# Cosine attention and a gated matmul pair: quad 3's transposes between M1's blocks, quad 4's ahead of quad 7's loads, the last tile in 512 and 256 columns

## Chip, cores, metric

One NeuronCore of one Trainium2 chip. The metric is device microseconds of one execution, the median of several runs. The profile is of one execution; its times count from the first instruction.

## The reference

```python
batch, n_heads, seq, head_dim = (8, 12, 448, 64)
n_tokens, d_model, d_ff = (3584, 768, 2048)

q_n = q / (np.linalg.norm(q, axis=-1, keepdims=True) + 1e-06)
k_n = k / (np.linalg.norm(k, axis=-1, keepdims=True) + 1e-06)
scores = np.matmul(q_n, k_n.transpose(0, 1, 3, 2)) / tau
scores = scores - np.max(scores, axis=-1, keepdims=True)
attn = np.exp(scores)
attn = attn / (np.sum(attn, axis=-1, keepdims=True) + 1e-09)
attn_out = np.matmul(attn, v)
x = attn_out.transpose(0, 2, 1, 3).reshape(B * S, H * D)   # 3584 x 768
h = x @ w_in                                               # 3584 x 2048
g = h * np.cos(h)
out = g @ w_out                                            # 3584 x 768
```

Inputs and output are float32.

## The kernel before

The twelve heads of a batch are taken four at a time; such a group is a *quad*, three to a batch, 24 in all. For a quad, q and k are loaded (`load_qk`, on SP's queue), squared and summed (`square`), turned into inverse norms (`inverse`: Ln and Exp on ScalarE, a reduce and a reciprocal on VectorE), scaled to bf16 (`scale`, into the single buffers `Qn` and `Kn`), and transposed into `qT` and `kT`. The first quads (0 to 3) are transposed on TensorE (`transpose`: seven 128x128 transposes into one PSUM bank, then one copy to SBUF on VectorE or ScalarE); from quad 4 on SP issues two transposing DMAs (`turn`). `scores` then makes one of seven groups of a quad's scores in a pair of PSUM banks, ScalarE takes the exponential into `E`, `attend` multiplies with v. The sums of E for quads 3 to 5 are spread over all partitions by a matmul (`spread`, L622) and inverted by Ln and Exp on ScalarE; later quads sum in rounds of two (`round_`, L661) and spread by DMA. The result is `xT`, the transposed input of the second half, one per batch.

The second half of a batch is M1 and M2. **M1** (`m1_part`, L707): eight pairs of 128 columns of `w_in`; each pair has two blocks of six matmuls of 448 columns, one block to a bank. `m1` then computes h cos h of the pair: ScalarE rounds h/2pi to an integer (L720), VectorE reduces the argument (L722), ScalarE takes the sine (L724), VectorE multiplies (L726) into `gT`. **M2** (`m2`, L735): a tile of 128 tokens has two halves of 384 output columns, each 16 matmuls, then one copy on VectorE (L744) and the store on SP (the last tile: on SP and ScalarE's queue, half by half).

The attention of later quads is spread over the M2 of a batch: `VISITS[c]` lists, for batch c, how many score or attend slots come next and how many M2 matmuls after them. `begin(qd)`, called at the first scores of a quad, normalises quad qd+2, turns it, loads quad qd+4 and squares quad qd+3.

TensorE's order is the order of the program (`key`, moved by `MOVE`; `FILL` puts small products on the identity into it, L846 and L850, at given operation numbers). Up to `P.strict = False` the order of the other engines is written out too. After that a planner chooses, at each free moment of an engine, among the instructions that are ready by its own durations: the one whose result TensorE needs first, with `lead` as an advantage in us. All waits are on semaphores by the tiles read and written; a PSUM bank is one such tile, so a writer waits for all readers of the whole bank. Two instructions marked `lock` are not planned at the same time.

W2 (`w_out`) is loaded in four chunks on GpSimd's queue (chunk i holds the blocks f = 4i to 4i+3 that M2 needs); `half[3]` holds the loads of the last two. PSUM has 8 banks: M1 of batch 0 uses, pair by pair, the banks `at_bank = 2, 0, 6, 4, 2, 6, 0, 4` and the one after each. The buffers for q and k in float32 are three each (quad modulo 3), `qT` and `kT` three each.

Of the kernel before, what the change touches and what calls it, by code (L numbers as in the profile page):

```python
# [21 lines left out]
class Planner:  # L22
# [81 lines left out]
    FILL = {24: [13, 1, 'f'], 42: [3, 1, 'f'], 56: [9, 1, 'q'], 137: [1, 6, 'q'], 139: [10, 6, 'q'], 141: [4, 2,  # L104
            'q'], 155: [6, 6, 'q'], 157: [5, 6, 'q'], 246: [2, 2, 'f'], 312: [1, 0, 'f']}
# [180 lines left out]
def bass_cosine_attention__then__act_gcu_kernel(  # L286
# [216 lines left out]
    def scale(qd, w, eng="pool", part=ALL[0]):  # L503
# [4 lines left out]
        return op(eng, (1.05 if eng == "dve" else 1.65) * (j1 - j0) / NJ,  # L508
                  lambda e: e.tensor_tensor(n[0].ap()[:, j0:j1].rearrange("p j r d -> p r j d"), f[s].ap()[:, :, j0:j1],  # L509
                                            rb, ALU.mult),  # L510
                  r=cut(nm + "f", s, part) + cut("rr%d" % w, u, part), w=cut(nm + "n", 0, part), lock=True)
# [19 lines left out]
    def transpose(qd, which, bk, part=ALL[0], eng="dve"):  # L531
        u = qd % 3
        j0, j1 = part
        n, t, nm = ((Qn, qT, "Q"), (Kn, kT, "K"))[which]

        def mm(e):
            for j in range(j0, j1):
                ins = e.transpose(PS.ap()[:, 512 * bk + 64 * j:512 * bk + 64 * j + 64].bitcast(BF16),
                                  n[0].ap()[:, j], ident.ap())
            return ins  # L540

        op("pe", 0.057 * (j1 - j0), mm, r=cut(nm + "n", 0, part) + ["ident"], w=whole(bk))
        src = PS.ap()[:, 512 * bk + 64 * j0:512 * bk + 64 * j1].bitcast(BF16)
        dst = t[u].ap()[:, j0:j1].rearrange("p j a x -> p (j a x)")
        if eng == "act":
            op("act", 0.13 + 0.067 * (j1 - j0), lambda e: e.activation(dst, src, ACT.Copy), r=whole(bk), w=cut(nm + "T", u, part))  # L546
            return
        op("dve", 0.07 + 0.067 * (j1 - j0), lambda e: e.tensor_copy(dst, src), r=whole(bk),
           w=cut(nm + "T", u, part))

    def turn(qd, after=()):

        u = qd % 3
        for n, t, nm in ((Qn, qT, "Q"), (Kn, kT, "K")):
            op("sp", 1.3, lambda e, n=n, t=t: e.dma_start_transpose(  # L555
                t[u].ap().rearrange("p j a x -> p j (a x)"), n[0].ap().rearrange("p j r d -> p (j r d)")),
               r=cut(nm + "n", 0, ALL[0]), w=cut(nm + "T", u, ALL[0]), dma=(nm + "T", u), moves=1.1, packet=18,
               after=after)

# [154 lines left out]
    def m1(c, pr, bk):  # L714
        s = pairs[0] % 3
        pairs[0] += 1
        col = S * (c % 2)
        bs = pair(bk)

        op("act", 0.815, lambda e: e.activation(ar[s].ap().bitcast(I32), two(bk), ACT.Identity, bias=0.25, scale=INV2PI),  # L720
           r=bs, w=[("ar", s)])
        op("dve", 1.005, lambda e: e.scalar_tensor_tensor(ar[s].ap(), ar[s].ap().bitcast(I32), -2.0 * math.pi, two(bk),  # L722
                                                          ALU.mult, ALU.add), r=bs + [("ar", s)], w=[("ar", s)])
        act("sin", 0.86, lambda e: e.activation(ar[s].ap(), ar[s].ap(), ACT.Sin, bias=GUARD * math.pi / 2.0, scale=GUARD),  # L724
            r=[("ar", s)], w=[("ar", s)])
        op("dve", 1.01, lambda e: e.tensor_tensor(gT.ap()[:, 2 * pr:2 * pr + 2, col:col + S], two(bk), ar[s].ap(), ALU.mult),  # L726
           r=bs + [("ar", s)], w=[("g", c % 2, 2 * pr), ("g", c % 2, 2 * pr + 1)])

    def m2(t, h, f0, f1, bk):
        col = 128 * t % GC  # L730
        bs = sorted({(128 * t) // S % 2, (128 * t + 127) // S % 2})

        def mm(e):
            for f in range(f0, f1):
                ins = e.matmul(bank(bk, HW), gT.ap()[:, f, col:col + 128], W2.ap()[:, f, HW * h:HW * h + HW],  # L735
                               start=(f == 0), stop=(f == NNB - 1))
# [4 lines left out]
        if f1 == NNB:
            so = t % 3
            end = t == B * S // 128 - 1
            op("dve", 0.475, lambda e: e.tensor_copy(osb[so].ap()[:, HW * h:HW * h + HW], bank(bk, HW)),  # L744
               r=whole(bk), w=[("o", so, h)])
            if end:
                store(t, HW * h, HW * h + HW, [("o", so, h)], ("sp", "act"))
# [35 lines left out]
    put_off = []  # L783

    def begin(qd):
# [5 lines left out]
        if qd < NQ - 4:  # L791
            steps.append(lambda after=(): load_qk(qd + 4, after))
# [329 lines left out]
```

## Time and profile before

| | |
|---|---|
| Median of 3 runs | 421.54 us (421.14 to 423.64) |
| Profiled execution | 422.46 us, span 420.6 us |
| TensorE busy | 410.1 us, 97% of the span |
| ScalarE, VectorE, GpSimd busy | 308.0, 271.6, 203.2 us |
| Matmuls M1 (L707) | 768, 146.8 us busy |
| Matmuls M2 (L735) | 896, 156.3 us busy |
| Read from HBM, written | 45.61 MB, 11.01 MB |

A row of a timeline gives the start in us, the length, the engine, the line of the kernel, the operation, what it writes and reads, its shape, how many are merged, and in brackets the idle time of the engine ahead of it with what ended that. PE is TensorE, PEld its weight loads, DVE is VectorE, ACT ScalarE, POOL GpSimd, SP SyncE; a q behind the name is that engine's queue. A row of groups gives busy time in us, the mean of one in ns, and the idle time ahead. The ends of matmuls are modelled, so that neighbours overlap a little.

M1 of batch 0 runs on TensorE from 35.02 us on, the visits of batch 0 from 59.34, M1 of batch 1 from 89.10.

### The profile page before, as it was taken

To read this page: it belongs to the slowest core of one execution; us is meant where nothing else is said; L and a number is where in the kernel's file an instruction comes from. 1 tells how busy PE (TensorE), PEld (TensorE's weight loads), DVE (VectorE), ACT (ScalarE), POOL (GpSimd) and SP (SyncE) were. 2 spreads that over 40 slices of the span, in tenths; PEclk is the share of its full clock that TensorE was granted. 3 is DMA by queue.
4 is the path that set the end of the run, shared out by engine and by line. 5 is a ranking of instruction groups with operands and counts; after the bars stand their busy time and mean duration, and the time that the engine had idled before them with its cause. 6 is when DMAs were issued, how large, how long until landed. Compare 5 with 4: busy or idle time off the path is not lost.

```text
span 420.6 us, 8751 instructions
## 1 busy us (share of the span) xinstructions
PE 410.1 (97%) x3700; PEld 219.2 (52%) x3700; DVE 271.6 (65%) x339; ACT 308.0 (73%) x412; POOL 203.2 (48%) x138
## 2 busy tenths in 40 slices
PE   7999999999999999999999999999999999999996
PEld 6564454445554455445555555454554555555563
DVE  5857796889863659845985469824883137836931
ACT  5998888988888977788788657789787747505700
POOL 2867337893286982689538763359303213000000
PEclk9999999999999999999999999999999999999999
DMA  8999999896099998499909991389605633031033
GB/s 261 230 241 210 232 216 250 210 206 153 2 204 167 246 258 221 73 191 205 258 25 206 183 269 40 61 145 228 144 0 83 134 71 86 2 75 39 1 75 76
DMA packets 71400, 62.84 MB, mean 149 GB/s; under 512 B 40512, under 2 KB 66368, under 8 KB 71360
## 3 DMA queue, kind: packets, MB, share of 16 engines
q1 hardware_dynamic: 60688, 50.09, 51.3%
q0 software_dynamic: 10240, 11.80, 17.4%
q8 instruction: 29, 0.48, 0.5%
q10 hardware_dynamic: 432, 0.39, 0.3%
q14 instruction: 11, 0.09, 0.1%
HBM read 45.61 MB, written 11.01 MB: 135 GB/s over the span
## 4 chain that ended last, share of the span: by engine, by line
PE 80%; DMA 11%; POOL 2%; DVE 2%; ACT 2%; SPq 1%; issue 1%
PE PS L735 33%; PE PS L707 30%; DMA W<-in_moe_w_out_dram 8%; PE PS L573 7%; PE PS L600 6%; PE PS L661 3%; DMA Qf<-in_q_dram 3%; SPq L555 1%; POOL E L461 1%; ACT E L581 1%; POOL W L436 1%; DVE n L465 1%; DVE AVs L609 1%; POOL sqq L461 0%; DVE osb L744 0%
## 5 line engine op out<-in xcount | busy, mean ns | idle before, releaser
L735 PE MATMUL PS<-W,gT 128*128 128x384 bf16 x896 | 156.3, 327 | 0.0
L581 ACT ACTIVATE E<-PS 128x896 bf16<-128x896 f32 x161 | 136.7, 917 | 20.0 <-PE PS L573 19.3
L707 PE MATMUL PS<-xT,W 128*128 128x448 bf16 x768 | 146.8, 353 | 0.3 <-ACT qT L546 0.3
L735 PEld LDWEIGHTS PS<-W,gT 128*128 128x128 bf16 x896 | 83.4, 98 | 69.4 <-issue 16.4
L707 PEld LDWEIGHTS PS<-xT,W 128*128 128x128 bf16 x768 | 74.7, 98 | 70.4 <-issue 0.6
L720 ACT ACTIVATE ar<-PS 128x896 int32<-128x896 f32 x64 | 58.2, 911 | 40.7 <-PE PS L707 40.5
L722 DVE SCALAR_TENSOR_TENSOR ar<-ar,PS 128x896 f32<-128x896 int32 x64 | 69.2, 1084 | 22.2 <-ACT ar L720 22.0
L726 DVE TENSOR_TENSOR gT<-PS,ar 128x896 bf16<-128x896 f32 x64 | 69.5, 1088 | 7.8 <-ACT ar L724 7.4
L744 DVE COPY osb<-PS 128x384 f32<-128x384 f32 x56 | 31.1, 555 | 65.1 <-PE PS L735 64.4
L724 ACT ACTIVATE ar<-ar 128x896 f32<-128x896 f32 x64 | 60.5, 947 | 15.4 <-DVE ar L722 15.2
L461 POOL TENSOR_TENSOR sqq<-Qf 128x896 bf16<-128x896 f32 x21 | 35.7, 1698 | 43.6 <-DVE n L465 30.2
L685 POOL TENSOR_TENSOR xT<-AVs,R 128x896 bf16<-128x896 f32 x17 | 35.5, 2088 | 41.4 <-DMA R<-Zs 41.3
L509 POOL TENSOR_TENSOR Qn<-Qf,rr 128x896 bf16<-128x896 f32 x21 | 37.9, 1806 | 32.5 <-DVE rr L501 21.4
L573 PE MATMUL PS<-qT,kT 64*64 64x448 bf16 x672 | 49.1, 358 | 2.6 <-ACT E L581 1.2
L461 POOL TENSOR_TENSOR sqk<-Kf 128x896 bf16<-128x896 f32 x21 | 37.3, 1778 | 8.0 <-DMA Kf<-in_k_dram 4.9
L600 PE MATMUL PS<-E,Vb 64*64 64x448 bf16 x672 | 37.7, 351 | 0.0
L609 DVE COPY AVs<-PS 128x896 f32<-128x896 f32 x21 | 22.9, 1090 | 19.5 <-PE PS L600 19.4
L465 DVE TENSOR_REDUCE n<-sqq 128x14 f32<-128x896 bf16 (+2 forms) x23 | 23.8, 1036 | 12.8 <-POOL sqq L461 12.0
L509 POOL TENSOR_TENSOR Kn<-Kf,rr 128x896 bf16<-128x896 f32 x18 | 30.4, 1687 | 0.6 <-DMA kT<-Kn 0.6
L573 PEld LDWEIGHTS PS<-qT,kT 64*64 64x64 bf16 x672 | 16.6, 105 | 26.4 <-issue 10.0
L421 POOL DMA_DIRECT2D Vb<-in_v_dram x24 | 17.9, 750 | 17.2 <-PE PS L573 11.8
L600 PEld LDWEIGHTS PS<-E,Vb 64*64 64x64 bf16 x672 | 19.2, 107 | 13.1 <-ACT E L581 1.8
(57 smaller groups left out, 212.8 us busy)
## 6 DMA issues: line engine op xcount, KB each, us to landing
out_dram<-osb SPq DMA_DIRECT2D x54, 192.0 KB, 3.3
Qf<-in_q_dram SPq DMA_DIRECT2D x23, 448.0 KB, 5.2
Kf<-in_k_dram SPq DMA_DIRECT2D x23, 448.0 KB, 5.4
R<-Zs SPq DMA_DIRECT2D x72, 112.0 KB, 3.5
Vb<-in_v_dram POOLq DMA_DIRECT2D x24, 224.0 KB, 7.0
W<-in_moe_w_in_dram POOLq DMA_DIRECT2D x4, 768.0 KB, 18.2
W<-in_moe_w_out_dram POOLq DMA_DIRECT2D x4, 768.0 KB, 26.8
qT<-Qn SPq DMA_TRANSPOSE x20, 4.3
```

The costliest lines, as they stand in the source:

```text
L461: op(eng, (1.68 if eng == "pool" else 1.05) * n, lambda e: e.tensor_tensor(dst, src, src, ALU.mult), r=cut(nm + "f", s, part), w=own, afte ...
L509: lambda e: e.tensor_tensor(n[0].ap()[:, j0:j1].rearrange("p j r d -> p r j d"), f[s].ap()[:, :, j0:j1], rb, ALU.mult),
L573: ins = e.matmul(bank(bs + r, S, 64 * a, 64 * a + 64), kT[u].ap()[64 * r:64 * r + 64, j, a, :], qT[u].ap()[64 * r:64 * r + 64, :, a, :], s ...
L581: act("exp", 0.81, lambda e: e.activation(E[es].ap(), two(bs), ACT.Exp, bias=0.0, scale=INV_TAU), r=pair(bs), w=[("E", es)], chain="E")
L600: ins = e.matmul(bank(bk + a, S, 64 * r, 64 * r + 64), Vb[vs].ap()[64 * a:64 * a + 64, r, j, :], E[es].ap()[64 * a:64 * a + 64, r, :], sta ...
L685: op(*(("dve", 1.05) if qd == 8 else ("pool", 2.04)), lambda e, u=u, sl=sl, b=b, c0=c0: e.tensor_tensor(xT[b % 2].ap()[:, c0:c0 + 2, :], A ...
L707: ins = e.matmul(bank(bk + i2), W1.ap()[:, i, 128 * nb:128 * nb + 128], xT[c % 2].ap()[:, i, :], start=(i == 0), stop=(i == NKC - 1))
L720: op("act", 0.815, lambda e: e.activation(ar[s].ap().bitcast(I32), two(bk), ACT.Identity, bias=0.25, scale=INV2PI), r=bs, w=[("ar", s)])
L722: op("dve", 1.005, lambda e: e.scalar_tensor_tensor(ar[s].ap(), ar[s].ap().bitcast(I32), -2.0 * math.pi, two(bk), ALU.mult, ALU.add), r=bs ...
L724: act("sin", 0.86, lambda e: e.activation(ar[s].ap(), ar[s].ap(), ACT.Sin, bias=GUARD * math.pi / 2.0, scale=GUARD), r=[("ar", s)], w=[("a ...
L726: op("dve", 1.01, lambda e: e.tensor_tensor(gT.ap()[:, 2 * pr:2 * pr + 2, col:col + S], two(bk), ar[s].ap(), ALU.mult), r=bs + [("ar", s)] ...
L735: ins = e.matmul(bank(bk, HW), gT.ap()[:, f, col:col + 128], W2.ap()[:, f, HW * h:HW * h + HW], start=(f == 0), stop=(f == NNB - 1))
```

## The change

Quad 3's transposes stood together ahead of pair 3's blocks, in pair 3's own banks, both copied by ScalarE. Now Q's stand between pair 2's blocks, in bank 4, copied by VectorE, and K's between pair 3's blocks, in bank 3, copied by ScalarE. Q of quad 3 is scaled on VectorE ahead of K on GpSimd, and the inverse norms of quad 4 come before both in the program, with a lead of 30; in M1 of batch 0 the last two steps of each pair have a lead of 1. Quad 4's transposing DMAs wait for the first of W2's last two chunks, no longer for both, and quad 7's loads wait until quad 4's K transpose has landed. The last tile's output is made as 512 and 256 columns. Further edits: `VISITS`, two `FILL` entries, the `MOVE` numbers that the reordering shifts.

```diff
-            119: 3.5, 197: 41.0, ...
+            119: 3.5, 197: 36.0, ...
-     ... 212: 17.5, 90: 3.5, 218: 4.0, 210: 5.5, ... 211: -2.0,
+     ... 210: 19.5, 90: 3.5, 218: 4.0, 208: 7.5, ... 209: -2.0,
-            'q'], 155: [6, 6, 'q'], 157: [5, 6, 'q'], 246: [2, 2, 'f'], 312: [1, 0, 'f']}
+            'q'], 155: [6, 6, 'q'], 157: [5, 6, 'q'], 312: [1, 0, 'f'], 342: [1, 6, 'q']}
...
-            op("act", 0.13 + 0.067 * (j1 - j0), lambda e: e.activation(dst, src, ACT.Copy), ...)
-            return
+            return op("act", 0.11 + 0.1 * (j1 - j0), lambda e: e.activation(dst, src, ACT.Copy), ...)
...
-    def m1(c, pr, bk):
+    def m1(c, pr, bk, after=()):
...
         act("sin", 0.86, lambda e: e.activation(ar[s].ap(), ...),
-            r=[("ar", s)], w=[("ar", s)])
+            r=[("ar", s)], w=[("ar", s)], lead=1.0 * (c == 0))
         op("dve", 1.01, lambda e: e.tensor_tensor(gT.ap()[:, 2 * pr:2 * pr + 2, col:col + S], two(bk), ar[s].ap(), ALU.mult),
-           r=bs + [("ar", s)], w=[("g", c % 2, 2 * pr), ("g", c % 2, 2 * pr + 1)])
+           r=bs + [("ar", s)], w=[("g", c % 2, 2 * pr), ("g", c % 2, 2 * pr + 1)], lead=1.0 * (c == 0))
...
     def m2(t, h, f0, f1, bk):
+        end = t == B * S // 128 - 1
+        x0, x1 = ((0, 512), (512, KM))[h] if end else (HW * h, HW * h + HW)
...
     VISITS = [
-        [(0, 25), (3, 12), (3, 12), (3, 4), (3, 4), (3, 12), (3, 10), (3, 3), (3, 4), (3, 0), (3, 4), (3, 5), (1, 1)],
-        [(0, 20), (3, 10), (3, 14), ... (3, 3), (3, 7), (1, 0)],
+        [(0, 25), (3, 12), (3, 11), (3, 3), (3, 5), (3, 12), (3, 10), (3, 4), (3, 4), (3, 0), (3, 4), (3, 5), (1, 1)],
+        [(0, 20), (3, 11), (3, 13), ... (3, 4), (3, 6), (1, 0)],
...
-        [(0, 19), (3, 9), (3, 12), (3, 14), (3, 0), (3, 24), (3, 6), (3, 17), (3, 7)],
-        [(0, 20), (3, 15), (3, 16), (3, 8), (3, 5), (3, 17), (3, 5), (3, 0), (3, 10)],
-        [(0, 18), (3, 13), (3, 13), (3, 12), (3, 0), (3, 24), (3, 17), (3, 17), (3, 0), (1, 14)],
+        [(0, 19), (3, 9), (3, 12), (3, 14), (3, 0), (3, 24), (3, 6), (3, 9), (3, 15)],
+        [(0, 20), (3, 15), (3, 16), (3, 8), (3, 5), (3, 16), (3, 6), (3, 0), (3, 10)],
+        [(0, 18), (3, 13), (3, 15), (3, 10), (3, 0), (3, 28), (3, 14), (3, 22), (3, 0), (1, 8)],
...
         if qd < NQ - 4:
-            steps.append(lambda after=(): load_qk(qd + 4, after))
+            steps.append(lambda after=turned if qd == FIRST else (): load_qk(qd + 4, after))
...
-    for w in range(2):
-        scale(FIRST, w)
+    mark = len(P.ops)
     for _ in inverse(FIRST + 1, 0, 2):
         pass
+    for o in P.ops[mark:]:
+        o.lead = 30.0
     P.strict = False
+    scaled = scale(FIRST, 0, "dve")
+    scaled.lead = 30.0
+    scale(FIRST, 1, after=[scaled])
     load_qk(FIRST + 3, half[3])
...
         for pr in range(NNB // 2):
+            blocks = order if pr < early else (0, 1)
+            if c == 0 and pr in (2, 3):
+                m1_part(c, pr, at_bank[pr], blocks[:1], 0, NKC)
+                transpose(FIRST, pr - 2, at_bank[pr + 1] + pr - 2, eng="dve" if pr == 2 else "act")
+                blocks = blocks[1:]
+            m1_part(c, pr, at_bank[pr], blocks, late if pr < early else 0, NKC)
+            m1(c, pr, at_bank[pr])
             if c == 0 and pr == 3:
                 for w in range(2):
-                    transpose(FIRST, w, at_bank[pr] + w, eng="act")
-                for w in range(2):
                     scale(FIRST + 1, w)
-                turn(FIRST + 1, half[3])
-            m1_part(c, pr, at_bank[pr], order if pr < early else (0, 1), late if pr < early else 0, NKC)
-            m1(c, pr, at_bank[pr])
+                turned += turn(FIRST + 1, half[3][:1])[1:]
```

More of the change, by code (lines that the diff above doesn't have):

```diff
@@ L501, in inverse, with scale @@
         op("dve", 0.3, lambda e: e.reciprocal(o, z), r=x, w=y, lead=lead)
-    def scale(qd, w, eng="pool", part=ALL[0]):
+    def scale(qd, w, eng="pool", part=ALL[0], after=()):
         s, u = qd % 3, qd % 2
@@ L510, in scale @@
                                             rb, ALU.mult),
-                  r=cut(nm + "f", s, part) + cut("rr%d" % w, u, part), w=cut(nm + "n", 0, part), lock=True)
+                  r=cut(nm + "f", s, part) + cut("rr%d" % w, u, part), w=cut(nm + "n", 0, part), lock=True, after=after)
     def cast(eng, part):
@@ L545, in transpose @@
         if eng == "act":
-            op("act", 0.13 + 0.067 * (j1 - j0), lambda e: e.activation(dst, src, ACT.Copy), r=whole(bk), w=cut(nm + "T", u, part))
-            return
+            return op("act", 0.11 + 0.1 * (j1 - j0), lambda e: e.activation(dst, src, ACT.Copy), r=whole(bk),
+                      w=cut(nm + "T", u, part))
         op("dve", 0.07 + 0.067 * (j1 - j0), lambda e: e.tensor_copy(dst, src), r=whole(bk),
@@ L553, in turn @@
         u = qd % 3
-        for n, t, nm in ((Qn, qT, "Q"), (Kn, kT, "K")):
-            op("sp", 1.3, lambda e, n=n, t=t: e.dma_start_transpose(
+        return [op("sp", 1.3, lambda e, n=n, t=t: e.dma_start_transpose(
                 t[u].ap().rearrange("p j a x -> p j (a x)"), n[0].ap().rearrange("p j r d -> p (j r d)")),
@@ L558, in turn @@
                after=after)
+                for n, t, nm in ((Qn, qT, "Q"), (Kn, kT, "K"))]
     summed = set()
@@ L720, in m1 @@
         op("act", 0.815, lambda e: e.activation(ar[s].ap().bitcast(I32), two(bk), ACT.Identity, bias=0.25, scale=INV2PI),
-           r=bs, w=[("ar", s)])
+           r=bs, w=[("ar", s)], after=after)
         op("dve", 1.005, lambda e: e.scalar_tensor_tensor(ar[s].ap(), ar[s].ap().bitcast(I32), -2.0 * math.pi, two(bk),
@@ L742, in m2 @@
             so = t % 3
-            end = t == B * S // 128 - 1
-            op("dve", 0.475, lambda e: e.tensor_copy(osb[so].ap()[:, HW * h:HW * h + HW], bank(bk, HW)),
+            op("dve", 0.475, lambda e: e.tensor_copy(osb[so].ap()[:, x0:x1], bank(bk, x1 - x0)),
                r=whole(bk), w=[("o", so, h)])
             if end:
-                store(t, HW * h, HW * h + HW, [("o", so, h)], ("sp", "act"))
+                store(t, x0, x1, [("o", so, h)], ("sp", "act"))
             elif h:
@@ L782, in bass_cosine_attention__then__act_gcu_kernel @@
     BEHIND = {10: 9}
-    put_off = []
+    put_off, turned = [], []
     def begin(qd):
```

4 lines of the change are left out of this document (2 added, 2 removed), and 10 rows, old and new, of tables (MOVE, VISITS).

## The prediction

> **What bounds the kernel now.** First the page's span and TensorE row, then the chain that ended last, then busy time by stretches.
>
> ```profile
> span 420.6 us, 8751 instructions
> ...
> PE 410.1 (97%) x3700; PEld 219.2 (52%) x3700; DVE 271.6 (65%) x339; ACT 308.0 (73%) x412; POOL 203.2 (48%) x138
> ```
> ```profile
> 344.27 18.16 PE PS L707 x96
> ...
> 396.26 20.81 PE PS L735 x128
> ```
> ```profile
> 55.18:89.10 33.92, 32.89 (x379) 15.94 (x378) 27.87 (x32) 32.08 (x45) 23.40 (x15) 1.00 1.07 209
> ...
> 107.26:396.30 289.04, 288.63 (x2483) 149.37 (x2482) 180.20 (x216) 212.68 (x274) 139.15 (x87) 1.00 0.62 132
> ```
>
> The lines that start with a stretch are from the third view; its columns are stretch, length, then busy time of TensorE, weight loads, VectorE, ScalarE and GpSimd. From 107.26 to 396.30 TensorE is idle for 289.04 - 288.63 = 0.41 us: nothing is to be had there but matmuls taken away, and the change takes none. From 55.18 to 89.10 (the visits of batch 0) it is idle for 1.03 us, and ScalarE is busy for 32.08 of 33.92, so there ScalarE is all but the bound too. From the chain, one M1 matmul (L707) goes out every 18.16/96 = 0.189 us, one M2 matmul (L735) every 20.81/128 = 0.163 us.
>
> The change's first part lies in M1 of batch 0. TensorE's timeline (start, length, engine, line, idle before):
>
> ```profile
> 35.02 6.98 PE L707 MATMUL PS<-xT,W 128*128 128x448 bf16 x36
> 41.84 0.55 PE L538 MATMUL PS<-ident,Qn 128*128 128x128 bf16 x7
> 42.23 0.55 PE L538 MATMUL PS<-ident,Kn 128*128 128x128 bf16 x7
> 43.22 0.28 PE L846 MATMUL PS<-ident 128*128 128x128 bf16 x2 [0.43 <-DVE gT L726]
> 43.82 11.52 PE L707 MATMUL PS<-xT,W 128*128 128x448 bf16 x60 [0.32 <-ACT qT L546]
> ```
>
> Seven transposes take 42.23 - 41.84 = 0.39 us, so the fourteen are issued by 42.62. Pair 3's matmuls write the banks that the transposes used, and start at 43.82, when ScalarE has emptied both. The hole is 43.82 - 42.62 = 1.20 us, the two fillers (L846) within it.
>
> **The hole, taken out.** The new order is: pair 2's first block, Q's transposes (bank 4), pair 2's second block, pair 3's first block (bank 4), K's transposes (bank 3), pair 3's second block (bank 5). Every user of a bank has a block of 6 x 0.189 = 1.13 us between itself and the next. What must be ready comes from VectorE, ScalarE and GpSimd (their timelines, and one group of instructions by shape: count, busy us, mean ns):
>
> ```profile
> 24.84 0.62 DVE L548 COPY qT<-PS 128x896 bf16<-128x896 bf16 x1
> ...
> 38.24 0.52 DVE L501 RECIPROCAL rr<-nrm 128x28 f32<-128x28 f32 x2
> 39.96 2.08 DVE L722 SCALAR_TENSOR_TENSOR ar<-ar,PS 128x896 f32<-128x896 int32 x2 [1.21 <-ACT ar L720]
> 42.07 1.09 DVE L726 TENSOR_TENSOR gT<-PS,ar 128x896 bf16<-128x896 f32 x1
> ...
> 57.33 2.19 DVE L726 TENSOR_TENSOR gT<-PS,ar 128x896 bf16<-128x896 f32 x2
> ```
> ```profile
> 43.65 0.92 ACT L546 ACTIVATE kT<-PS 128x896 bf16<-128x896 bf16 x1
> ...
> 58.42 1.28 ACT L381 ACT_TABLE_LOAD   x1
> ```
> ```profile
> 38.66 1.68 POOL L509 TENSOR_TENSOR Qn<-Qf,rr 128x896 bf16<-128x896 f32 x1 [2.50 <-DVE rr L501]
> 40.31 1.68 POOL L509 TENSOR_TENSOR Kn<-Kf,rr 128x896 bf16<-128x896 f32 x1
> ```
> ```profile
> L509 DVE TENSOR_TENSOR Qn<-Qf,rr 128x896 bf16<-128x896 f32 x2 | 2.2, 1089 | 0.0
> ```
>
> Q's scale on VectorE takes 1.09 us and runs from 38.76, in the 1.21 us in which VectorE waits for ScalarE: it ends at 39.85, before L722 starts at 39.96, and costs nothing; were that idle time gone, it would cost VectorE its 1.09. GpSimd then scales K from about 39.95 to 41.63, earlier than now (41.99). TensorE issues Q's transposes at 35.02 + 30 x 0.189 = 40.70, done with drain at 41.26 (0.55 us each). VectorE has done pair 0's L722 at 41.00, copies Q in 0.62 to 41.9, and takes pair 0's L726 at 42.07 as now. Pair 3's first block is due at 40.70 + 0.39 + 1.13 = 42.23: bank 4 is free. K's transposes follow at 43.37; bank 3 needs pair 0's L726, over at 43.16. ScalarE's copy of K (0.92) then ends near 44.9, and bank 3 is written next by pair 4's second block, at 46.04. Nothing waits, and M1 ends 1.20 us earlier, at 53.98. The edits to the planner's numbers (durations, leads, the renumbered MOVE entries, and 197's, whose instruction stays the last of ScalarE's strict line) only decide this order and cost nothing themselves. Bounds: 0.6 saved if Q's copy goes behind pair 1's L722 (second rival), 1.20 at best.
>
> **The visits of batch 0.** M2 and scores start 1.20 us sooner, but ScalarE's exponentials wait for its table load at 58.42, which follows pair 7's sine. VectorE has 16 M1 instructions of about 1.07 us and the copy of 0.62 from 39.96 on, 17.7 us in all, so its last L726 ends no sooner than 57.7 (now 59.5). With the whole 1.20 it ends at 58.3; I allow it up to 0.6 us of waiting more, 58.9. So ScalarE starts 0.6 to 1.2 us earlier; I take 0.8. Then the waits within the stretch (TensorE's and ScalarE's timelines):
>
> ```profile
> 65.77 0.57 PE L573 MATMUL PS<-qT,kT 64*64 64x448 bf16 x8 [0.37 <-issue]
> ...
> 71.34 0.57 PE L573 MATMUL PS<-qT,kT 64*64 64x448 bf16 x8 [0.22 <-DVE AVs L609]
> ...
> 83.05 1.52 PE L622 MATMUL PS<-E,ones 64*64 64x448 bf16 x28 [0.42 <-ACT E L581]
> ```
> ```profile
> 68.59 0.92 ACT L635 ACTIVATE ar<-PS 128x896 f32<-128x896 f32 x1 [0.61 <-PE PS L622]
> ```
> And SP's timeline, the DMA view of narrow windows (last column: us from issue to landing), and both for W2's chunks 1 and 2 on GpSimd's queue:
>
> ```profile
> 45.63 0.47 SPq L409 DMA_DIRECT2D Kf<-in_k_dram  x1
> ...
> 46.66 0.47 SPq L409 DMA_DIRECT2D Kf<-in_k_dram  x1
> 56.30 1.34 SPq L555 DMA_TRANSPOSE qT<-Qn  x1
> 57.69 3.52 SPq L555 DMA_TRANSPOSE kT<-Kn  x1
> 61.26 0.59 SPq L409 DMA_DIRECT2D Qf<-in_q_dram  x1
> ```
> ```profile
> Kf<-in_k_dram SPq DMA_DIRECT2D x1, 448.0 KB, 14.8
> ...
> Kf<-in_k_dram SPq DMA_DIRECT2D x1, 448.0 KB, 11.0
> ...
> kT<-Kn SPq DMA_TRANSPOSE x1, 8.0
> ```
> ```profile
> 19.85 1.51 POOL L436 DMA_DIRECT2D W<-in_moe_w_out_dram  x2
> ...
> W<-in_moe_w_out_dram POOLq DMA_DIRECT2D x2, 768.0 KB, 26.8
> ```
>
> Quad 5's K is issued at 45.63 and lands 11.0 us later, at 56.6; quad 7's K, at 46.66, 14.8 later, at 61.5; quad 4's K transpose, at 57.69, 8.0 later, at 65.7, just when the scores at 65.77 start: TensorE waits there for it. The transposes were held until 56.30 by W2's last chunk. Afterwards they wait for the chunk before it. Chunks 1 and 2 land 26.8 us after issue on average; chunk 1 was there when SP went on at 45.22, 25.4 after its issue at 19.85, so chunk 2 takes 28.2 and lands at 48.8. SP then issues both transposes by about 54, behind quad 5's loads alone (56.6). The same 4.2 us that lie now between quad 7's K and quad 4's kT put kT at 60.8, and scores want it near 64. Quad 7's loads wait for kT, quad 6's for the last chunk; whichever SP takes first, both are issued by about 62, where quad 6's now go at 61.26. So quad 7's come some 6 us later than now, and what reads them on GpSimd runs behind quad 6's squares. The stores of tile 0 follow on SP with less than 1 us of delay; the output buffers are three.
>
> The 0.37 us at 65.77 goes, and with it most of ScalarE's 0.61 at 68.59, which is the same delay seen on the spread. I take 0.7 of ScalarE's idle time as won. With the 0.8 that makes 1.5 us at the end of the visits. Bounds: 0.6 (an earlier start alone) to 1.20 + 1.03 = 2.2 (all of TensorE's idle time of the stretch).
>
> The new filler (ahead of operation 342, two small products into bank 6) costs about 0.1, and it has to wait until VectorE has emptied bank 6; VectorE has quad 5's K scale in front of that, so 0 to 0.6; I take 0.15. The one taken out stood in the hole.
>
> **Visits of later batches.** The lists move M2 matmuls to other gaps and take none away. Gain at most 0.41 (above), loss about the same by the largest such waits; I take 0.
>
> **The last tile.**
>
> ```profile
> L744 DVE COPY osb<-PS 128x384 f32<-128x384 f32 x56 | 31.1, 555 | 65.1 <-PE PS L735 64.4
> ...
> L609 DVE COPY AVs<-PS 128x896 f32<-128x896 f32 x21 | 22.9, 1090 | 19.5 <-PE PS L600 19.4
> ```
> ```profile
> out_dram<-osb SPq DMA_DIRECT2D x1, 192.0 KB, 2.6
> ...
> out_dram<-osb SPq DMA_DIRECT2D x1, 96.0 KB, 2.2
> out_dram<-osb ACTq DMA_DIRECT2D x1, 96.0 KB, 2.4
> ```
>
> The copies give (1090 - 555)/512 = 1.045 ns an element, so 256 columns save 0.13 us. Halving a store from 192 to 96 KB saved 0.4, so a further 32 KB saves about 0.13. Matmuls of 448 and 384 columns go out every 0.189 and 0.163, 0.41 ns a column, so 512 and 256 together cost what two of 384 do. Saved: 0.27, from 0.1 (the copy alone) to 0.4.
>
> **Sum.** -1.5 + 0.15 + 0 - 0.27 = -1.62 us. The profiled execution took 422.46 with a span of 420.6; it would become 420.84 with a span of 419.0. It lies 0.92 above the median of 421.54, which becomes 419.9. Bounds of the terms together: from -0.2 to -2.9, which is 418.6 to 421.3.
>
> **Rivals.** *ScalarE keeps the time* (419.9 becomes 421.0): TensorE arrives early and waits for exponentials, since 32.08 of 33.92 us are ScalarE's. For it: 0.42 us at 83.05 waits for E. Against: ScalarE itself idles 0.61 on TensorE. Then only its earlier start of 0.6 and the tail count, less 0.3 for the filler: 0.55.
>
> *Q's copy does not come when meant* (420.5): VectorE takes pair 1's L722 first, 41.0 to 42.04, the copy ends at 42.7 and pair 3's first block starts at 42.8 instead of 42.23: 0.57 lost. Against it: the planner prefers what TensorE needs soonest, and that is the copy.
>
> *W2's last chunk comes late, and the kernel is slower* (422.5). Quad 4's transposes now run while this chunk is in flight. TensorE needs it at the 25th M2 matmul: 53.98 + 24 x 0.163 = 57.9; it lands at 56.3, so 1.6 us are free. If the transposes take their whole 4.2 us out of it, it lands at 60.5 and TensorE stands for 2.6: -1.62 + 2.6 = +1.0. It decides from a landing at 59.5 on. Against: while quad 5's loads ran beside it the chunk got through as well. The Trainium skill, in DMA: Bandwidth & Descriptors, Queues, rings and completion order, says that each DMA engine takes turns between queue rows packet by packet. By that rule the chunk, on GpSimd's row, keeps its turns whatever SP's row carries, so the sum stays at -1.62 instead of +1.0; this trace has SP's row busy beside the chunk, but with no transposes.
>
> *All of it is won* (418.5): the stretch's whole 1.03, the 0.41 later, and 0.4 at the end: 1.20 + 1.03 + 0.41 + 0.4 = 3.0. Against: E at 83.05.
>
> **How the numbers follow.** Forecast 0.55 (own range 418.9 to 420.6), ScalarE 0.18, late copy 0.10, late chunk 0.09, all won 0.08. 1% is 4.2 us, about what a measurement of this kernel tells from no change. All idle time that I can name sums to 3.0, so faster by over 1% needs something unnamed: 0.04, out of the last case. Slower by over 1% needs a chunk over 5 us late: 0.03, out of the late chunk. Same: 0.93. The range from 417.7 to 422.3 adds to the bounds most of the late chunk's case and the spread of the runs (421.14 to 423.64).
>
> **What would show it.** Right: no L538-to-L707 hole over 0.3 us in M1 of batch 0; M2's first matmul near 54.0; table load before 58.0; quad 4's transposes issued near 49 and 50, landed by 61; no wait at the 65.77 scores; the last matmul of M1 of batch 1 about 1.5 us earlier; last copy 0.42 us. Wrong: TensorE waiting for W2 after 25 M2 matmuls, for gT in pairs 5 to 7, or new waits over 0.5 us after 107.

## The result, and the profile after

| | before | after |
|---|---|---|
| Median of 22 runs each | 421.52 us (421.14 to 426.35) | 420.53 us (419.63 to 422.89) |
| Ratio, 95% interval | | 0.9965 (0.995 to 0.998) |
| Profiled execution, span | 422.46, 420.6 us | 419.94, 418.1 us |
| M1 of batch 0 starts | 35.02 | 34.77 |
| M1 start to M2 start, batch 0 | 20.16 | 19.08 |
| M2 start to M1 of batch 1 (the visits) | 33.92 | 33.05 |
| Last copy, and from its end to the end of the span | 0.56, 2.98 | 0.42, 2.79 |

The gain is 0.35%, or 0.0035 x 421.5 = 1.48 us (0.84 to 2.11). The ratio lies near that of the means (420.68 to 422.02 us, 0.9968), in which single long executions such as the 426.35 of before count; the medians alone differ by only 0.99 us. The two profiled executions differ by 2.52 us, a whole microsecond more than the ratio says, so the pair of profiles cannot be read as the effect of the change. The experiments below say which part of their difference is the change.

The page of after (span, TensorE's row), then its busy time by stretch (stretch, length, busy time of TensorE, weight loads, VectorE, ScalarE, GpSimd; then TensorE's granted clock, DMA share, GB/s):

```profile
span 418.1 us, 8752 instructions
...
PE 410.2 (98%) x3700; PEld 219.8 (53%) x3700; DVE 272.6 (65%) x341; ACT 307.2 (73%) x411; POOL 201.7 (48%) x137
```
```profile
34.77:53.85 19.08, 19.08 (x115) 10.03 (x111) 17.30 (x21) 16.02 (x21) 7.65 (x6) 1.00 1.15 228
53.85:86.90 33.05, 32.62 (x380) 16.04 (x380) 27.39 (x32) 32.25 (x45) 23.58 (x14) 1.00 1.06 217
105.10:394.00 288.90, 288.60 (x2482) 149.35 (x2481) 179.90 (x216) 212.76 (x273) 138.89 (x87) 1.00 0.63 132
```

TensorE's own work has not changed (410.2 against 410.1 us). The first row shows no idle time: 19.08 of 19.08 (a wait of 0.13 us at its end, below, is hidden by the modelled ends). From 105.10 on it idles for 0.30 us, as good as the 0.41 of before. TensorE's timeline of after:

```profile
34.77 5.85 PE L707 MATMUL PS<-xT,W 128*128 128x448 bf16 x30
40.45 0.55 PE L538 MATMUL PS<-ident,Qn 128*128 128x128 bf16 x7
40.84 2.43 PE L707 MATMUL PS<-xT,W 128*128 128x448 bf16 x12
43.11 0.55 PE L538 MATMUL PS<-ident,Kn 128*128 128x128 bf16 x7
43.50 10.38 PE L707 MATMUL PS<-xT,W 128*128 128x448 bf16 x54
53.85 4.24 PE L738 MATMUL PS<-W,gT 128*128 128x384 bf16 x25
...
63.52 0.82 PE L573 MATMUL PS<-qT,kT 64*64 64x448 bf16 x12
```

No row carries a bracket, where before had 0.43 and 0.32: each group of transposes takes its 0.39 us and a block follows at once. VectorE's and ScalarE's timelines beside it:

```profile
38.35 1.09 DVE L509 TENSOR_TENSOR Qn<-Qf,rr 128x896 bf16<-128x896 f32 x1
...
41.04 0.62 DVE L548 COPY qT<-PS 128x896 bf16<-128x896 bf16 x1 [0.25 <-PE PS L538]
...
51.60 2.19 DVE L726 TENSOR_TENSOR gT<-PS,ar 128x896 bf16<-128x896 f32 x2
```
```profile
43.70 0.92 ACT L546 ACTIVATE kT<-PS 128x896 bf16<-128x896 bf16 x1 [0.61 <-PE PS L538]
...
56.96 1.28 ACT L381 ACT_TABLE_LOAD   x1
```

Q's copy runs as soon as the transposes are drained. M1's last matmuls go out at 43.50 + 54 x 0.189 = 53.71, yet M2 starts at 53.85, just behind VectorE's second L726, over at 51.60 + 2.19 = 53.79: M2's first bank is the one that this L726 reads. SP's timeline, and the DMA view of a narrow window around the issue of quad 4's second transpose (last column: us to landing):

```profile
48.41 1.33 SPq L554 DMA_TRANSPOSE qT<-Qn  x1
49.79 5.67 SPq L554 DMA_TRANSPOSE kT<-Kn  x1
55.51 0.59 SPq L409 DMA_DIRECT2D Qf<-in_q_dram  x1
...
61.69 0.37 SPq L409 DMA_DIRECT2D Qf<-in_q_dram  x1
```
```profile
kT<-Kn SPq DMA_TRANSPOSE x1, 11.9
```

Quad 4's transposes go out 7.9 us earlier than before, but the K transpose takes 11.9 us instead of 8.0 and lands at 61.7. The end of the kernel, VectorE's last copy and the last two stores:

```profile
414.92 0.42 DVE L746 COPY osb<-PS 128x256 f32<-128x256 f32 x1 [1.05 <-PE PS L738]
```
```profile
out_dram<-osb SPq DMA_DIRECT2D x1, 64.0 KB, 2.0
out_dram<-osb ACTq DMA_DIRECT2D x1, 64.0 KB, 2.2
```

### The profile page after: what moved, and what is told of

Same layout as the page of the kernel before. It is cut to its first block, busy times and chain, and to the rows that moved or that the text cites. A ratio compares the mean times of both kernels' runs of the same rounds, so it can differ in the third digit from the quotient of the medians.

```text
span 418.1 us, 8752 instructions
## 1 busy us (share of the span) xinstructions
PE 410.2 (98%) x3700; PEld 219.8 (53%) x3700; DVE 272.6 (65%) x341; ACT 307.2 (73%) x411; POOL 201.7 (48%) x137
## 4 chain that ended last, share of the span: by engine, by line
PE 91%; ACT 6%; DVE 1%; DMA 1%; issue 0%
PE PS L738 36%; PE PS L707 35%; PE PS L573 8%; PE PS L600 7%; PE PS L661 3%; ACT E L581 3%; PE PS L622 1%; ACT E L588 1%; DMA Kf<-in_k_dram 1%; ACT ar L639 1%; ACT ar L635 1%; DVE n L465 1%; PE PS L538 0%; DVE osb L746 0%; DVE Qn L509 0%; PE PS L848 0%
## 5 line engine op out<-in xcount | busy, mean ns | idle before, releaser
L738 PE MATMUL PS<-W,gT 128*128 128x384 bf16 (+2 forms) x896 | 156.3, 327 | 0.0
L726 DVE TENSOR_TENSOR gT<-PS,ar 128x896 bf16<-128x896 f32 x64 | 69.5, 1088 | 6.9 <-ACT ar L724 6.4
L746 DVE COPY osb<-PS 128x384 f32<-128x384 f32 (+2 forms) x56 | 31.1, 556 | 62.7 <-PE PS L738 61.9
L509 POOL TENSOR_TENSOR Qn<-Qf,rr 128x896 bf16<-128x896 f32 x20 | 37.0, 1848 | 28.2 <-DVE rr L501 23.1
L465 DVE TENSOR_REDUCE n<-sqq 128x14 f32<-128x896 bf16 (+2 forms) x23 | 23.8, 1036 | 14.9 <-POOL sqq L461 14.2
L465 DVE TENSOR_REDUCE n<-sqk 128x14 f32<-128x896 bf16 (+2 forms) x23 | 23.8, 1037 | 4.3 <-POOL sqk L461 4.1
```

Source lines behind the costliest of these rows:

```text
L465: return op("dve", 0.07 + 0.95 * n, lambda e: e.tensor_reduce(out=n2.ap()[:, u, H * w:H * w + H] if part == ALL[0] else jr(n2, u, w, part) ...
L738: ins = e.matmul(bank(bk, x1 - x0), gT.ap()[:, f, col:col + 128], W2.ap()[:, f, x0:x1], start=(f == 0), stop=(f == NNB - 1))
```

## Experiments

Two stretches are followed through all of them, for the start of M1 of batch 0 itself moves between 34.5 and 38.0 us from profile to profile: *M1 to M2* (from M1's first matmul to M2's first, batch 0) and *the visits* (from there to the first matmul of M1 of batch 1).

**The first part alone (e1_m1_only).** Before, with the transposes between the blocks, the scale of Q on VectorE and the new leads; loads, transposing DMAs, visits, fillers of the visits and last tile as before. Against after:

```diff
-                turned += turn(FIRST + 1, half[3][:1])[1:]
+                turn(FIRST + 1, half[3])
-            'q'], 155: [6, 6, 'q'], 157: [5, 6, 'q'], 312: [1, 0, 'f'], 342: [1, 6, 'q']}
+            'q'], 155: [6, 6, 'q'], 157: [5, 6, 'q'], 312: [1, 0, 'f']}
...
```

> The first part alone on the kernel before: quad 3's transposes between M1's blocks in other banks, Q scaled on VectorE, the leads; quad 4's transposes still wait for both of W2's last chunks, the visits and the last tile are as before. Theory A (the parts depend on each other): the hole closes, M2 of batch 0 starts 1.1 us earlier, but the scores of quad 4 still wait for its kT, which lands near 65.7 as before; TensorE stands there for about 1.4 us instead of 0.37, and the start of M1 of batch 1 comes only 0 to 0.5 us earlier; median 421.0 to 421.6. Theory B (the parts add): M1 of batch 1 starts 1.1 us earlier, median 420.4.

Measured: 421.04 against 421.62 us, ratio 0.9977 (0.9965 to 0.999). The visits of its profile, and TensorE at quad 4's scores:

```profile
53.79:86.88 33.09, 32.63 (x378) 15.93 (x378) 27.49 (x32) 32.17 (x45) 24.84 (x15) 1.00 1.08 221
```
```profile
63.63 0.76 PE L573 MATMUL PS<-qT,kT 64*64 64x448 bf16 x12
```

M1 to M2 is 19.08, as in after, and the visits take 33.09: the whole 1.08 us arrives at M1 of batch 1. The scores of quad 4 do not wait, although the transposes are still held by W2's last chunk (kT lands at 63.44). The theory that the earlier start would be lost again in a longer wait for kT falls; the parts add.

**Quad 4's part alone (e2_quad4_only).** Before, with these lines:

```diff
...
-                turn(FIRST + 1, half[3])
+                turned += turn(FIRST + 1, half[3][:1])[1:]
...
-            steps.append(lambda after=(): load_qk(qd + 4, after))
+            steps.append(lambda after=turned if qd == FIRST else (): load_qk(qd + 4, after))
```

> The second part alone on the kernel before: quad 4's transposes wait for one chunk of W2, quad 7's loads for quad 4's kT. The hole in M1 stays at 1.20 us. Theory A: kT lands near 61.7, the wait of 0.37 us at the scores of quad 4 and ScalarE's 0.61 behind it go, M1 of batch 1 starts 0.6 to 0.9 us earlier; median 420.7 to 421.0. Theory B (ScalarE bounds the stretch from its table load on, whatever TensorE waits for): under 0.3 us earlier, median 421.3 or more.

Measured: 421.57 us, ratio 1.002 (0.9989 to 1.0052): no difference is shown. The median of before is 421.62; the ratio is above 1 because three of the twelve executions took 425.05 to 426.52. M1 to M2 is 20.16 again. The visits:

```profile
56.66:89.75 33.09, 32.63 (x379) 16.00 (x378) 27.22 (x32) 32.07 (x45) 22.22 (x14) 1.00 0.93 208
```

The visits are 0.83 shorter than in the profile of before, and kT lands at 61.2; by itself that would look like a gain of this part. But e3 and e5, in which SP does what it did before, show the same 33.09.

**The last tile alone (e3_tail_only).** Before, with the new `m2` only.

> The last tile alone as 512 and 256 columns on the kernel before. Theory A: last copy 0.42 us instead of 0.56 and 0.13 to 0.2 us less from the copy's end to the end of the span, 0.3 us in all in the profile; the medians are too close to tell. Rival: the first half's larger stores (128 KB to a queue) are still under way and hold the last ones back, no gain.

Measured: 421.44 us, ratio 0.9984 (0.9971 to 0.9996). The copy takes 0.42 us instead of 0.56, and from its end to the end of the span it is 2.81 instead of 2.98: 0.31 us in all. Its stretches:

```profile
35.30:55.46 20.16, 19.41 (x116) 10.23 (x113) 15.64 (x19) 16.83 (x22) 9.64 (x8) 1.00 1.15 234
55.46:88.55 33.09, 32.63 (x379) 15.92 (x377) 27.23 (x32) 32.07 (x45) 23.27 (x14) 1.00 0.99 207
```

**After, profiled again (e4_after_again)**, with no edit.

> The changed kernel unaltered, for a second profile: the first pair of profiles differ by 2.5 us in span, the medians by 1.0. Theory A: 0.25 us of the 2.5 is the start of M1 of batch 0 (35.02 against 34.77), set by the first loads, and varies from one execution to the next; from the start of M1 of batch 0 to the start of M1 of batch 1 the second profile again takes 52.1 us (54.1 before), and what differs between executions lies ahead of 35 us. Rival: executions differ within the visits of batch 0, where transfers and engines meet, and this stretch takes 52 to 54 us.

Measured: 419.91 us, ratio 0.9963 (0.9949 to 0.9977); M1 to M2 19.08, the visits 33.06.

**Before, profiled again (e5_before_again)**, with no edit.

> The kernel before unaltered, for a second profile. In the first one W2's last chunk landed at 56.3 and TensorE waited for quad 4's kT; in the run of the last tile alone, whose batch 0 is the same, the chunk landed at 53.9 and there was no such wait. Theory A (the wait is of one execution, not of the kernel): from the start of M1 of batch 0 to that of batch 1 53.25 us as in that run (54.1 in the first profile), no wait at the scores of quad 4. Rival: 54.1 us again, and the run of the last tile alone was the odd one.

Measured: 421.94 against 421.84 us, ratio 1.0013 (0.9989 to 1.0038).

```profile
38.00:58.16 20.16, 19.41 (x116) 10.24 (x113) 15.64 (x19) 16.84 (x22) 10.98 (x8) 1.00 1.15 243
58.16:91.25 33.09, 32.63 (x379) 15.99 (x378) 27.23 (x32) 32.07 (x45) 21.91 (x13) 1.00 0.96 182
```

So the unchanged kernel also needs only 33.09 us for the visits. The 33.92 of the profile from which the prediction was made, with its 0.37 us at 65.77 and its 0.61 on ScalarE, belonged to that one execution. In it W2's last chunk landed at 56.29 and with it quad 4's kT at 65.67, 30.7 us behind the start of M1; here they land at 54.32 and 64.17, 26.2 behind, and in e3, where M1 starts at 35.30 as in before, at 53.93 and 63.40, 28.1 behind. In all other profiles the chunk lands between 53.6 and 55.7.

**After without quad 4's part (e6_no_quad4):** `turn(FIRST + 1, half[3])` again, the rest as after.

> The changed kernel with quad 4's transposes waiting for both chunks again and quad 7's loads free. Theory A (the SP part is worth something only when the chunk is late): the stretch from M1 to M1 stays at 52.1 us when the chunk lands before 55.1 (kT then by 63.5, scores at 63.7); the median is 0 to 0.4 us above the changed kernel's, out of executions with a late chunk. Theory B (the SP part is worth the 0.7 us of the forecast): 52.8 us or more, median 0.7 us above.

Measured: 421.17 us, ratio 0.9978 (0.995 to 1.0007); M1 to M2 19.08, the visits 33.05, as in after. Its median is 0.64 above after's, but the intervals overlap, and the stretch that this part could shorten is the same. In the profiles quad 4's part is worth nothing. It may be a safeguard: in e1, without it, kT landed at 63.44, 8.35 us behind the chunk, and the scores came at 63.63, only 0.19 us later. By these numbers a chunk at 56.29, as in the profile of before, would put kT at 64.6 and cost up to about 1 us; that is an estimate, and no run shows it.

**The transposes in the next block's bank (e8_own_banks):** after, with the transposes between the blocks but each in the bank that the next block writes.

```diff
-                transpose(FIRST, pr - 2, at_bank[pr + 1] + pr - 2, eng="dve" if pr == 2 else "act")
+                transpose(FIRST, pr - 2, at_bank[pr] + 1, eng="dve" if pr == 2 else "act")
```

> The changed kernel with the transposes at the same places between the blocks, but in the bank that the very next block writes (7 and 5 instead of 4 and 3). Theory A (the other banks are what closes the hole): each next block waits for its copy: Q's ends near 41.7 where the block is due at 40.84, 0.9 us; K's (ScalarE, 0.92 us) near 44.6 where the block is due at 43.5, 1.1 us; M1 2.0 us longer than in the changed kernel, the median 1 to 2 us above it, at or above the kernel before. Rival: the place alone is enough, under 0.5 us lost.

Measured: 423.42 us, ratio 1.0034 (1.002 to 1.0047). TensorE:

```profile
41.83 2.44 PE L707 MATMUL PS<-xT,W 128*128 128x448 bf16 x12 [0.72 <-DVE qT L548]
...
45.67 10.39 PE L707 MATMUL PS<-xT,W 128*128 128x448 bf16 x54 [1.01 <-ACT kT L546]
56.59 4.24 PE L738 MATMUL PS<-W,gT 128*128 128x384 bf16 x25 [0.53 <-DVE gT L726]
```

Each block now waits for the copy out of its own bank (0.72 and 1.01 named; 0.89 and 1.18 against after's positions). So the place between the blocks alone does not close the hole; the other banks are needed. Other banks without the new place were not run. The 0.53 at M2 is VectorE's: its planned order put quad 5's L465 ahead of the L726 that M2's bank waits for.

**Q's scale on GpSimd (e7_q_on_pool, e10_q_pool_lead5, e12_q_pool_same).** In e7 both scales go to GpSimd without a lead; e10 is e7 with the lead of M1's last steps at 5 instead of 1; e12 is after, with the engine of this one instruction changed only once the order of every engine has been planned.

```diff
-    scaled = scale(FIRST, 0, "dve")
-    scaled.lead = 30.0
-    scale(FIRST, 1, after=[scaled])
+    for w in range(2):
+        scale(FIRST, w)
```
```diff
         self.plan()
-        self.waits()
+        self.moved.eng = "pool"; self.waits()
...
-    scaled.lead = 30.0
+    scaled.lead = 30.0; P.moved = scaled
```

> The changed kernel with Q of quad 3 scaled on GpSimd as before, ahead of K; the transposes stay between the blocks. Theory A (VectorE's scale only makes room): GpSimd has Q at 40.3 and K at 42.0 as in the kernel before, TensorE wants them at 40.45 and 43.1, so TensorE's M1 is the same within 0.1 us; median as the changed kernel's within 0.2. Rival: Q comes some 0.1 to 0.4 us late for the transposes, and VectorE's copy of Q meets pair 0's and 1's steps in another order; M1 0.3 us longer or more.

> The changed kernel with Q of quad 3 scaled on GpSimd, and the lead of M1's last two steps 5 instead of 1, so that the planner no longer puts quad 5's square sum among M1's steps on VectorE. Theory A (the 2.6 us that the run with Q on GpSimd lost came from that order alone: VectorE stood 1.57 us for a load in the middle of M1): M1 of batch 0 takes 18.9 to 19.2 us from its first matmul to M2's again, and the median is the changed kernel's, within 0.3 us of 420.2. Rival (Q has to be on VectorE): 0.5 us or more longer.

> After, with quad 3's scale of Q put back on GpSimd ahead of K's, and nothing else: every engine keeps after's order of instructions (the two earlier tries on GpSimd, q_on_pool and q_pool_lead5, changed the planned order too). In after's profile the inverse norm of Q is there at 38.32; GpSimd would scale Q from about 38.45 in 1.68 us to 40.1, K from there to 41.8, and TensorE issues Q's transposes at 40.45 and K's at 43.11. Theory A (what the earlier tries lost was the order alone, the engine of the scale does not matter): transposes at the same distance from M1's start as in after (5.68 and 8.34 us), M1's start to M2's start 19.0 to 19.3 us, to M1 of batch 1 about 52.1 to 52.3, no wait over 0.2 us in M1 of batch 0, median as after's, 419.9 to 420.6, ratio near 0.997. Rival (VectorE's 1.09 us instead of GpSimd's 1.68 is needed): Q is ready 0.2 to 0.6 us late, a wait of that size ahead of Q's transposes, M1's start to M2's start 19.4 to 19.8, median 420.5 to 421.0.

Measured: e7 422.87 us, ratio 1.0025 (1.0006 to 1.0044); e10 421.16, 0.9996 (0.9972 to 1.002); e12 420.61, 0.9965 (0.9937 to 0.9993). First e7's TensorE and VectorE, then e10's TensorE, then e12's TensorE and GpSimd:

```profile
43.07 0.55 PE L538 MATMUL PS<-ident,Kn 128*128 128x128 bf16 x7
...
47.59 6.98 PE L707 MATMUL PS<-xT,W 128*128 128x448 bf16 x36 [0.57 <-DVE gT L726]
56.34 4.24 PE L738 MATMUL PS<-W,gT 128*128 128x384 bf16 x25 [1.76 <-DVE gT L726]
```
```profile
54.20 1.09 DVE L465 TENSOR_REDUCE n<-sqq 128x14 f32<-128x896 bf16 x1 [1.57 <-POOL sqq L461]
```
```profile
46.51 8.12 PE L707 MATMUL PS<-xT,W 128*128 128x448 bf16 x42 [0.81 <-ACT kT L546]
```
```profile
40.34 0.55 PE L538 MATMUL PS<-ident,Qn 128*128 128x128 bf16 x7
40.73 2.43 PE L707 MATMUL PS<-xT,W 128*128 128x448 bf16 x12
...
53.74 2.45 PE L738 MATMUL PS<-W,gT 128*128 128x384 bf16 x14
```
```profile
38.29 1.68 POOL L509 TENSOR_TENSOR Qn<-Qf,rr 128x896 bf16<-128x896 f32 x1 [2.50 <-DVE rr L501]
40.05 1.69 POOL L509 TENSOR_TENSOR Kn<-Kf,rr 128x896 bf16<-128x896 f32 x1
```

In e7 the transposes are on time (43.07 - 34.72 = 8.35 us behind M1's start, 8.34 in after). What is lost, 2.54 us of M1 to M2, is order: VectorE waits 1.57 us for a square that was planned to be there and then runs quad 5's L465 ahead of the L726 that M2 needs. No theory had that. In e10 ScalarE takes two sines ahead of K's copy (0.81 at 46.51; M1 to M2 20.12). With the order held, e12, all is as in after: M1 to M2 19.08, the visits 33.05, the ratio the same. The engine of Q's scale is worth nothing; Q is ready at 38.29 + 1.68 = 39.97 and wanted at 40.34.

**Less work on ScalarE (e11_no_exp):** after, without the Exp of the inverse sums of quads 3 to 5.

```diff
         def exp():
+            if qd in DIRECT:
+                return
             act(...
```

> The changed kernel without the Exp of the inverse sums of quads 3 to 5 (three ScalarE instructions of 0.95 us; the output is scaled wrongly for these quads). From ScalarE's table load to the start of M1 of batch 1 all profiles but one show 29.8 to 30.0 us. Theory A (ScalarE bounds this stretch): it becomes 28.7 to 29.4 us, TensorE's wait of 0.42 near 80.85 goes; median 0.6 to 1.2 us below the changed kernel's. Rival (TensorE's own work bounds it): 29.8 us and the same median.

Measured: 428.16 us, ratio 1.0147 (1.013 to 1.0163). The visits of batch 0 and TensorE within them:

```profile
53.60:86.52 32.92, 32.34 (x381) 15.77 (x381) 27.31 (x32) 30.21 (x42) 23.06 (x13) 1.00 1.04 217
```
```profile
80.56 1.52 PE L622 MATMUL PS<-E,ones 64*64 64x448 bf16 x28 [0.51 <-ACT E L581]
```

ScalarE is busy for 30.21 us here and 32.25 in after: 2.04 less, and the stretch is shorter by 0.13. ScalarE, busy for 98% of after's stretch, does not set its length; TensorE's own 32.3 to 32.6 us do. Even the wait for E is still there. The total is no measure of this: from M1 of batch 1 to M1 of batch 7 the kernel takes 297.90 us, against 288.61 in e4. One late K transpose costs 3.8 of these 9.3 us, by the group of the scores that wait for it (busy us, mean ns, idle time ahead and its cause):

```profile
L573 PE MATMUL PS<-qT,kT 64*64 64x448 bf16 x144 | 10.8, 366 | 4.0 <-DMA kT<-Kn 3.8 <-issue 0.2
```

Where the rest goes was not followed.

**A wait against a stretched instruction (e9_port_wait):** after, with GpSimd's square of quad 1's K held until VectorE has scaled quad 0's Q; the last section tells why.

```diff
-    for part in HALVES:
-        scale(0, 0, "dve", part)
+    halves = [scale(0, 0, "dve", part) for part in HALVES]
...
-    add1 = [square(1, 1, "pool", after=[kept])]
+    add1 = [square(1, 1, "pool", after=[kept, *halves])]
```

> The changed kernel with one wait more: GpSimd's square of quad 1's K waits until VectorE has scaled quad 0's Q; no engine's order changes. In the profiles in which M1 of batch 0 starts at 36.5 to 38.0, GpSimd starts that square at 8.9 to 9.2 us, 0.4 us into VectorE's second scale of Q, which then takes 2.6 to 2.7 us instead of 0.68, and quad 3's loads are issued at 11.2 to 11.5 instead of 9.1 to 9.5; in the profiles with a start at 34.5 to 35.3 GpSimd starts at 9.4 or later, after the scale. Theory A: the wait keeps every execution in the second kind; the changed kernel's median of 419.9 to 420.5 becomes 419.4 to 419.9, its executions spread less, hardly one above 420.8. Rival: early and late starts come from the loads themselves; the spread and the median stay.

Measured: 420.25 us (419.53 to 422.23), ratio 0.9964 (0.9942 to 0.9986), which is after's ratio. The spread of the runs stays, so this was inconclusive: whatever the wait removes, it is not what makes most of the spread. The profiled execution, one of the longer ones (421.79), lost its time further on. In the visits TensorE waits at the new filler for VectorE's copy out of the bank:

```profile
65.88 0.24 PE L852 MATMUL PS<-ident 64*64 64x128 bf16 x2 [0.38 <-DVE osb L746]
```

The visits take 33.50 us here, and M1 of batch 2 to M1 of batch 3, with a wait of 0.89 us at the scores at 187.09, takes 47.91 against 46.89 in e4. Apart from the profile of before (33.92) and e8 (33.84, with other waits), the visits take 32.92 to 33.09 us in all other profiles.

## Why the prediction was right or wrong

419.9 us was predicted and 420.53 measured; against the median of before the sum was -1.62 us, the ratio says -1.48. That the total is so near is in part luck: of the sum's terms one was 0.70 us too much, the others together 0.50 too little.

*The hole.* Predicted 1.20 us, measured 20.16 - 19.08 = 1.08. M1's matmuls do end 1.20 earlier; "nothing waits" was wrong by 0.13, since M2's first bank is that of VectorE's L726, over at 53.79. In e7 and e8, too, M2 starts 0.06 us behind the end of that L726. e8 shows that without the other banks the blocks wait, as the prediction said. VectorE's 1.09 us for Q's scale cost nothing, as costed, and e12 shows that they also buy nothing.

*What reaches the end of the visits.* This term is mis-sized: ScalarE was called all but the bound there, and 0.8 of the 1.20 us were to arrive because its table load was allowed up to 0.6 of waiting more for VectorE. That waiting did not come: the load is 23.41 - 22.20 = 1.21 us earlier counted from M1's start. All 1.08 arrive (visits 33.09 in e1 and 33.09 in e3 and e5). With the load so early they would have arrived with ScalarE as the bound as well; that it is not the bound is shown by e11.

*The 0.7 us of waits won.* This step failed. They were there to be read, but in one execution alone: e5 and e3 take 33.09 us with no such waits although SP does there what it did before, and e2, with the change on SP, takes the same. In the pair of profiles the term seems to come true (33.92 to 33.05), and just this is the trap. 0.8 + 0.7 = 1.5 was predicted for the end of the visits; 1.08 + 0 is what the change does.

*Filler and visits.* Priced at 0.15, the filler costs nothing in after: the visits take 33.05 with it and 33.09 without (e1). In e9 TensorE waited 0.38 us at it, within the 0 to 0.6 that the prediction allowed; whether the products behind it would have waited as well was not run. The lists later on: from M1 of batch 1 to M1 of batch 7 it is 288.76 us before and 288.79 after, from there to the last copy 39.23 in both: the 0 that was taken. By the test of a second execution this is no more than "nothing seen": that stretch takes 288.61 in e4 and 290.33 in e5, where TensorE stands 1.44 us for a late K transpose in batch 2.

*The last tile.* Predicted 0.27, measured 0.31 in e3: 0.14 from the copy, 0.17 behind it.

*The sum as measured* is 1.08 + 0.03 (the visits, before rounding) + 0.31 = 1.42 us, within the ratio's 0.84 to 2.11. The lower end of the prediction's bounds, -0.2, does not follow from its terms: 0.6 - 0.6 - 0.41 + 0.1 saves -0.31, a loss of 0.3 us; the measured gain is far from either. The profiled pair has 2.52: 1.94 up to M1 of batch 1, of which 0.83 is the one late execution, 0.25 from the start of M1, and 0.33 at the end.

*Quad 4 on SP.* Issue at 48.41 and 49.79 (predicted 49 and 50); landing at 61.7, where "by 61" was said: the K transpose took 11.9 us, not the time that it had beside quad 7's K. SP was also held 5.67 us by that one issue, so quad 6's loads go out at 55.51, 5.8 earlier than before, and quad 7's at 61.69, as predicted.

*Rivals.* ScalarE keeps the time: fell with e1 and e11. Q's copy late: fell, pair 3's first block starts 7.2 us behind M1's start as worked out. W2's last chunk late: fell; with the transposes beside it, it landed at 54.48 and 54.06 (in the variants between 53.6 and 55.7), without them between 53.8 and 56.3, and TensorE does not wait for it. The rule of packet turns in the Trainium skill (DMA: Bandwidth & Descriptors, Queues, rings and completion order) agrees with that. All of it won: fell, since the 0.3 to 0.4 us of idle time in the visits and later stayed.

## What to carry to other kernels

A wait in one profiled execution is a term of the sum only if a second execution of the same kernel has it too: here 0.7 of 1.5 us were of that one run, and comparing two single profiles would have confirmed them. A busy share of 98% does not make an engine the bound: here taking 2.04 us of work from ScalarE shortened the stretch by 0.13, and the gain ahead of it passed whole. When a PSUM bank is borrowed between two blocks of matmuls, choose it so that a whole block lies between the borrower and the next writer, and hold the order of the other engines while trying such an edit: two variants here (e7 and e10) lost 2.5 and 1.0 us by order alone, and e8 0.5 of its 2.6.

## What had not been expected of the hardware

The start of M1 of batch 0 lies between 34.5 and 38.0 us in the profiles; the unchanged kernel alone has 35.02 and 38.00. In the three profiles with the latest starts (e2 36.50, e5 38.00, e6 37.89) one instruction was stretched: the second part of VectorE's scale of quad 0's Q. It and GpSimd's square, first in e4 (M1 from 34.54), then in e5 (M1 from 38.00):

```profile
8.36 0.68 DVE L509 TENSOR_TENSOR Qn<-Qf,rr 128x512 bf16<-128x512 f32 x1
```
```profile
9.80 1.70 POOL L461 TENSOR_TENSOR E<-Kf 128x896 bf16<-128x896 f32 x1
```
```profile
8.76 2.68 DVE L509 TENSOR_TENSOR Qn<-Qf,rr 128x512 bf16<-128x512 f32 x1
```
```profile
9.20 1.69 POOL L461 TENSOR_TENSOR E<-Kf 128x896 bf16<-128x896 f32 x1
```

In these three GpSimd's square starts 0.39 to 0.47 us into VectorE's instruction, which takes 2.64 to 2.72 us instead of 0.68; GpSimd's 1.69 stay, and SP issues quad 3's load between 11.15 and 11.47, in the other profiles between 9.07 and 9.94. Where GpSimd starts after VectorE's end, or within 0.08 us of it (e11), nothing is stretched. The Trainium skill (SBUF — State Buffer, SBUF: two separate sides) says that whichever of the two starts first holds the shared pair of ports for its whole instruction and the other one blocks. By the starts in these rows VectorE was first and was the one held up, against that order. Elsewhere the order holds, as at quad 5's scales within the visits, VectorE's K and GpSimd's Q, first in after, then in e9:

```profile
62.12 1.09 DVE L509 TENSOR_TENSOR Kn<-Kf,rr 128x896 bf16<-128x896 f32 x1
```
```profile
62.16 2.59 POOL L509 TENSOR_TENSOR Qn<-Qf,rr 128x896 bf16<-128x896 f32 x1 [5.35 <-DVE rr L501]
```
```profile
62.79 2.56 DVE L509 TENSOR_TENSOR Kn<-Kf,rr 128x896 bf16<-128x896 f32 x1 [0.15 <-DMA kT<-Kn]
```
```profile
62.72 1.69 POOL L509 TENSOR_TENSOR Qn<-Qf,rr 128x896 bf16<-128x896 f32 x1 [4.92 <-DVE rr L501]
```

The one that starts first keeps its time (1.09, 1.69), the other takes 2.59 and 2.56; in e9 this held up VectorE's next copy, for which the filler waited. Over all 14 profiles a VectorE product of two SBUF tiles starts ahead of one on GpSimd and runs beside it for over 0.15 us in 113 places: in 110 of them GpSimd's takes over 2 us instead of about 1.7, and the other three are those of e2, e5 and e6. Why these went the other way is open.

The stretched instruction is not the whole of a late start. In e5 and e6 TensorE's granted clock fell as well. The stretch from 12 to 24 us, in e2, then in e5 (the third number from the end is the clock):

```profile
12.00:24.00 12.00, 11.42 (x194) 7.23 (x189) 9.52 (x17) 11.34 (x24) 7.93 (x9) 1.00 1.08 230
```
```profile
12.00:24.00 12.00, 11.81 (x183) 7.92 (x183) 9.61 (x15) 10.22 (x21) 7.93 (x10) 0.86 1.06 223
```

In e6 it is 0.88, in all other profiles 1.00. M1 starts at 38.0 and 37.9 in e5 and e6, but at 36.50 in e2, which has the stretched instruction at the full clock. What lowered the clock is not shown. From 8 to 12 us TensorE was busy for 1.08 us in e5 and 1.16 in e6, for 1.42 in e2, and for 3.1 to 3.5 in the profiles without the stretched instruction, so that idle time ahead of the drop is the nearest candidate. e9, which keeps the two instructions apart, could not tell: M1 started at 35.32 there, but neither its 12 executions nor after's 34 (e4's included) had a mean granted clock below 0.998.
